# Order of the turns on SyncE's queue and the packet size of four v chunks in a fused attention and mixer kernel

## The chip, the cores and the metric

The kernel runs on one core of a Trainium2 chip. The metric is the device time of one execution in microseconds (us). A core has five engines that run their own instruction streams: TensorE (PE, with its weight loads PEld), VectorE (DVE), ScalarE (ACT), GpSimd (POOL) and SyncE (SP), which only issues transfers here. The transfers run on 16 DMA engines. In the profile the transfers that POOL issues are queue q0 (software_dynamic) and those that SP issues are queue q1 (hardware_dynamic).

## What is computed

Batch is 8, the sequence S is 3008, the model width is 256, the width of z is 64. First a gated attention without softmax, then a mixer over tokens and over channels:

```python
scores = (1.0 / S) * np.matmul(z, z.transpose(0, 2, 1))
attn = np.maximum(scores, 0.0) ** 2
x = u * np.matmul(attn, v)                       # S x 256 for each batch
h = np.maximum(x.transpose(0, 2, 1) @ w_tok1, 0.0) @ w_tok2
u2 = x + h.transpose(0, 2, 1)
out = u2 + np.maximum(u2 @ w_ch1, 0.0) @ w_ch2
```

Inputs and output are float32; the kernel computes in bf16 with float32 sums.

## The kernel before

**Tiles.** The sequence is cut into 24 tiles of 128 rows and these into 6 chunks of 4 tiles (`NG` = 6, `GK` = 4; the last chunk, `LAST` = 5, is short: 3 tiles and 64 rows). A block (b, q) is the attention of 512 query rows of batch b (`NQ` = 6 blocks for a batch). A block goes through 6 groups: group g multiplies the squared scores of 512 queries and key chunk g with chunk g of v. So the whole attention is a sequence of steps, numbered (b * NQ + q) * NG + slot; step 12 is the first group of the third block of batch 0.

**Scores.** PE makes scores (L457) in pairs of key tiles, ACT takes them out of PSUM with the ReLU into a tile named `at` (L495), DVE squares them in place (L503). There are 6 buffers for `at`. In batch 0 every block makes all its own scores. From batch 1 on, a score block off the diagonal is made once and used twice: as it is for block q, and turned, for block g. Turning it (a "flip", L554) is a transposing DMA on SP's queue from `at` to a tile named `fl`. An `at` buffer is free again once PE and its flip have read it.

**Turning by DMA.** SP also issues the transposing DMAs that turn z (`turn_z`, L141 and L145, from `zs` to `zT`; three for the second half), u (`turn_u`, L258, from `ur` to `uT`) and the gated result x (`turn_x`, L875, from `xT` to `x_pair`). The first chunks of batch 0's z are turned on PE, but chunks 2 and 3 by DMA (`turn_first_z`, L150, from `zr` to `zT`). SP takes its queue strictly in order, and each instruction waits there for what it needs. `turn_x` of block (b, q) needs the block's end: PE's sums, added and multiplied by u on DVE (L818, L838).

**Loading.** POOL issues every load that has to become bf16: v (L220), u (L248), z (L129), the weights w_tok1 (L267), w_tok2 (L277) and w_ch (L284, L289). POOL takes its queue in order, too. A one-column copy to a scratch tile (`after`, L124) serves as a gate: POOL stops at it until the named column has been written. One such gate stands ahead of the loads of batch 1's v, of all weights and of two chunks of u; it waits for the last column of batch 1's turned z (`zTs[1][:, KT, :1]`).

**v of batch 0.** It lies in three buffers of the ring `fl` (11 buffers, shared with `ur` and `uT` of batch 0's later blocks and with the flips). Buffer c // 2 holds chunks c, one after the other, so that each partition's part of a chunk, 4 rows of 256 bf16, is one run of 2 KB in the destination. `release("fl", ...)` counts a buffer free when both of its chunks have been used in batch 0's last block.

**Order.** Under a manual schedule the program writes instructions in the order that a planner in Python finds while the kernel is built. It keeps a clock for PE (`pe[0]`), ACT, DVE and SP with estimated durations, and at each turn picks the piece of work that can start first. `at_group(n, f)` hangs a load or a turn on step n: f is written out when the planner reaches that step. SP's part in it is `on_sp` and `push("sp", ...)`; the time that loads take from SP's transfers is guessed by `loading` and `shared`. The planner is not told how transfers share the DMA engines. The DVE sums of the mixer (`x_sums`, L912, that read `x_pair`; `token_sums`, L956, that read w_tok1) are pushed at estimated times after the turns and loads that they need.

On SP's queue, up to batch 1's flips, the written order before the change is: u(0,1), x(0,0), first half of batch 1's z (step 12), u(0,2) (step 13), x(0,1), u(0,3) and second half of z (step 14), u(0,4), u(0,5) (steps 15 and 16), x(0,2), and so on. The gate on POOL and the loads behind it start at step 15.

Of the kernel before, what the change touches and what calls it, by code (L numbers as in the profile page):

```python
# [9 lines left out]
BF16 = mybir.dt.bfloat16  # L10
# [3 lines left out]
P = 128  # L14
QW = 512
GK = 4
# [41 lines left out]
def kernel(  # L58
# [12 lines left out]
    B, S, D = u.shape  # L71
# [9 lines left out]
    NQ = (S + QW - 1) // QW  # L81
    NG = KT // GK
    LAST = NG - 1
# [4 lines left out]
    sb = ctx.enter_context(tc.tile_pool(name="sb", bufs=2))  # L88
# [25 lines left out]
    def rows_of(ap, c):  # L114

        n = full_tiles[c]
        return ap[c * QW:c * QW + n * P, :].rearrange("(p t) d -> p t d", t=n)

    def last_rows(ap):
        return ap[(KT - 1) * P:, :]  # L120
# [67 lines left out]
    def bank_pair(slot, name):  # L188

        if slot == RING and not last_psum:  # L190
            first.close()
            last_psum.append(ctx.enter_context(
                tc.tile_pool(name="last_psum", bufs=1, space=bass.MemoryType.PSUM)))
        pool = psum if slot < RING else last_psum[0]
        return pool.tile([P, 2, QW], F32, tag=f"ps{slot}", name=name, bufs=1)
# [12 lines left out]
    def load_v(b, c):  # L208
        if b == 0:

            if c // 2 not in v_first:
                v_first[c // 2] = sb.tile(
                    [P, 2, GK, D], BF16, tag="fl", name="v_sb", bufs=ROOM["fl"])
                live["fl"] += 1
                fl_free.pop(0)
            vt = v_first[c // 2][:, c % 2]
        else:
            vt = sb.tile([P, GK, D], BF16, tag="v", name="v_sb", bufs=NG)
        n = full_tiles[c]
        nc.gpsimd.dma_start(out=vt[:, :n, :], in_=rows_of(v[b], c))  # L220
        if n < GK:
            for r in range(2):
                nc.gpsimd.dma_start(
                    out=vt[r * TAIL:(r + 1) * TAIL, n, :], in_=last_rows(v[b]))
        vs[b, c] = vt
        v_in[b, c] = Done(pe[0] + 9.0 if b > 1 else 0.0)
        loading(LOAD)

    v_first, v_uses = {}, [[2] for _ in range(NG // 2)]

# [104 lines left out]
    def loading(us):  # L335
        loads[0] = max(loads[0], pe[0] + 1.0) + us
# [8 lines left out]
    ROOM = {"at": 6, "fl": 11, "xT": 9, "h2": 6, "us": 2}  # L345
# [48 lines left out]
    pe = [0.0]  # L394
# [164 lines left out]
    def release(name, uses, t=0.0):  # L559
        uses[0] -= 1  # L560
        uses[1:] = [max([t] + uses[1:])]
        if not uses[0]:
            live[name] -= 1
            if name == "at":
                at_free.append(uses[1])
            if name == "fl":
                fl_free.append(uses[1])
# [37 lines left out]
    def finished(blk, g):  # L605
        blk.parts[g] -= 1
        if not blk.parts[g]:
            _, _, name, uses = blocks.pop((blk.b, blk.q, g))
            release(name, uses, pe[0] + 0.2)
            if blk.b == 0 and blk.q == NQ - 1:  # L610
                release("fl", v_uses[g // 2], pe[0] + 0.2)

    def tails_ready(blk):

# [27 lines left out]
    def do_whole(start, g):  # L642
        blk = cur[0]
        begins = blk.g is None
        if begins:
            blk.g, blk.half = g, 0
            blk.todo.remove(g)
            blk.slot += 1
            blk.parts.setdefault(g, 2 if g == LAST else 1)
            n = grain(blk.b, blk.q, g)  # L650
            tiles = list(range(GK - 1 if g == LAST else GK))
            blk.steps = [(dh, tiles[i:i + n]) for i in range(0, GK, n) for dh in range(DT)]
        final = blk.slot == NG
        if begins:
            if final and not blk.tails:
                do_tails(blk, max(start, tails_ready(blk)))
                start = pe[0]
        dh, tiles = blk.steps[blk.half]
        start, end = on_pe(start, "full", len(tiles) * column_time(blk.W))
        for i in tiles:  # L660
            whole_matmul(blk, g, i, dh, final and i == tiles[-1])
        if final:
            acc_free[dh] = push(
                "dve", end + 0.21, 0.61, 0.75,
                lambda t, dh=dh: gate(blk, dh, blk.acc[dh], t), first=1,
                room=("xT",) if dh == 0 else lambda: (blk.b, blk.q) in xTs)
        blk.half += 1
        if blk.half == len(blk.steps):
            blk.g = None
            finished(blk, g)  # L670
            if final:
                end_block(blk)
                if blk.q == WHOLE - 1:
                    ring.append((acc_free[-1], RING))
# [71 lines left out]
    def do_half(start, g):  # L746
        blk = cur[0]
        if blk.whole:
            return do_whole(start, g)
        if blk.g is None:  # L750
            start_bundle(blk, g, start)
        g, dh, tiles = blk.steps[blk.half]
        blk.half += 1
        final = dh is not None and blk.slot == NG and not any(
            d == dh or d is None for _, d, _ in blk.steps[blk.half:])
        if dh is not None and blk.acc[dh] is None:
            blk.home[dh], free_at = take_slot()
            blk.acc[dh] = bank_pair(blk.home[dh], f"acc{dh}")
            start = max(start, free_at)
        start, end = on_pe(start, "half", len(tiles) * column_time(blk.W))  # L760
        for i in tiles:
            for h in range(2):
                av_matmul(blk, g, i, h if dh is None else dh, h, final and i == tiles[-1])
        if final:
            finish(blk, dh, end)
        if blk.half == len(blk.steps):
            blk.g = None
            for g in blk.bundle:
                _, _, name, uses = blocks.pop((blk.b, blk.q, g))
                release(name, uses, pe[0] + 0.2)  # L770
                used[blk.b, g] = used.get((blk.b, g), 0) + 1
                if blk.b == 0 and blk.q == NQ - 1:
                    release("fl", v_uses[g // 2], pe[0] + 0.2)
            if blk.slot == NG:
                end_block(blk)

# [154 lines left out]
    def take_slot():  # L931
        slot = min((s for s in ring if s[0].t is not None), key=lambda s: s[0].t)
        ring.remove(slot)
        return slot[1], slot[0].t
# [574 lines left out]
    def turn_next_z(b, half):  # L1509
        turn_z(zTs[b + 1], half)  # L1510
        on_sp(2.8 + 1.2 * half)

        for c in range(NG // 2 * half, NG // 2 * (half + 1)):
            turned[b + 1, c] = Done(pe[0] + 10.0)
        if half:
            turned[b + 1, NG // 2 - 1] = Done(pe[0] + 10.0)
# [4 lines left out]
    def at_group(n, f):  # L1521
        fetch.setdefault(n, []).append(f)
# [45 lines left out]
    for b in range(B):  # L1568
        base = b * NQ * NG
        for q in range(NQ):  # L1570
            m = b * NQ + q + 2
            if b == 0:
                if m < NQ:
                    at_group(base + NG, lambda m=m: load_u(m // NQ, m % NQ))
                late_turn = NQ * NG + 1 + 4 * (m - NQ) if m >= NQ else 2 * NG + (1, 2, 3, 4)[q]
                at_group(base + late_turn, lambda m=m: turn_u(m // NQ, m % NQ))
            elif m < 2 * NQ:
                ask_u(m, base + q * NG + 2)
        if b == 0:
            at_group(base + 2, lambda b=b: new_zT(b + 1))  # L1580
            for j in range(NG):
                at_group(base + 3 + j // 2, lambda b=b, j=j: load_z(b + 1, j))
                if j % 3 == 2:
                    at_group(base + 12 + 2 * (j // 3), lambda b=b, j=j: turn_next_z(b, j // 3))
        else:
            if b == 1:
                ask_z(2, base + HALF * NG - 1)
            if b + 1 < B:
                last, m = base + NQ * NG - 1, (b + 1) * NQ
                ask_u(m, last)  # L1590
                for j, c in enumerate(vorder):
                    at_group(last, lambda b=b, c=c, j=j: when_used(b, c, j))
                ask_u(m + 1, last)
                ask_u(m + 2, last)
                if b + 2 < B:
                    ask_z(b + 2, last)
                for k in range(3, NQ):
                    ask_u(m + k, last)
# [66 lines left out]
    items += [lambda c=c: ask_w_tok2(c) for c in range(NG)]  # L1665
    items += [lambda part=part: ask_w_ch(part) for part in range(4)]
    items += [lambda m=m: load_u(m // NQ, m % NQ) for m in (NQ, NQ + 1)]
    begin = 2 * NG + 3
    at_group(begin, lambda: after(zTs[1][:, KT, :1]))
    for k, item in enumerate(items):  # L1670
        at_group(begin + k * (NQ * NG - NG - begin + 1 + W_LATER) // len(items), item)
# [33 lines left out]
    while cur[0] is not None or heads or tails:  # L1705
        run_engines(pe[0])
        ask_some()
        t = pe[0]
        ta, g = next_half(t)
# [133 lines left out]
```

## Times and profile before

| | |
|---|---|
| time, median of 3 runs | 1132.12 us (1129.81 to 1133.4) |
| the profiled execution | 1130.13 us, of which 1128.3 are its span |
| PE busy | 1112.0 us, 99% of the span |
| DVE busy | 782.6 us, 69% |
| ACT busy | 654.1 us, 58% |
| POOL busy | 162.9 us, 14% |
| transferred | 165.52 MB, mean 147 GB/s |

Rows of a timeline give start, duration, engine, line, operation, tiles and count, and in brackets the idle time of the engine just before with what ended it. SPq rows are DMA issues: their start is when the queue came to them, their duration is the issue, not the transfer. "DMA to landing" is the time from an issue to its data's arrival (least, median, most). A row of a view by windows has the stretch, then busy time and count of each engine (PE, PEld, DVE, ACT, POOL), then the granted PE clock, then the busy share of the DMA engines (over 1 where packets overlap) and GB/s. A queue's row has packets, MB and the share of the 16 engines' time.

### The profile page before, as it was taken

The numbers are of one execution on the slowest core, as the hardware profiler recorded it, in microseconds if no ns is written. First come the engines' busy times: TensorE is split into PE (matmuls) and PEld (weight loads), VectorE is DVE, ScalarE is ACT, GpSimd is POOL, SyncE is SP. The second block draws the span as 40 slices with busy tenths as digits, with TensorE's granted clock in tenths as the row PEclk, the third lists the DMA queues.
The fourth block names the chain that finished last, engine by engine and source line by source line (L and its number), as shares of the span: only waits on it lengthen the run. The fifth ranks groups of instructions, "written<-read, shape, count | busy, mean of one in ns | idle before, by whom it ended". The sixth has DMA issues, their size and how long they took to land.

```text
span 1128.3 us, 26908 instructions
## 1 busy us (share of the span) xinstructions
PE 1112.0 (99%) x10965; PEld 676.1 (60%) x10965; DVE 782.6 (69%) x1849; ACT 654.1 (58%) x817; POOL 162.9 (14%) x388
## 2 busy tenths in 40 slices
PE   8999999999999999999999999999999999999998
PEld 3444465666557665576555765557655576556676
DVE  6888756875767757578566785667756777557774
ACT  7997535535855358545665456753666526753353
POOL 4140010221002110022100320003110120000000
PEclk9999999999999999999999999999999999999999
DMA  9699965688977879879697896957969779594223
GB/s 171 97 200 193 199 129 118 112 156 165 180 143 131 163 149 183 139 145 186 141 149 143 143 198 133 190 112 136 201 145 161 127 145 175 135 164 97 61 65 87
DMA packets 464620, 165.52 MB, mean 147 GB/s; under 512 B 433072, under 2 KB 446960, under 8 KB 464496
## 3 DMA queue, kind: packets, MB, share of 16 engines
q1 hardware_dynamic: 436640, 131.11, 58.2%
q0 software_dynamic: 27344, 32.32, 20.5%
q8 instruction: 85, 1.39, 0.5%
q10 hardware_dynamic: 512, 0.38, 0.1%
q14 instruction: 39, 0.32, 0.1%
HBM read 65.40 MB, written 24.64 MB: 80 GB/s over the span
## 4 chain that ended last, share of the span: by engine, by line
PE 89%; DVE 5%; DMA 4%; ACT 1%; issue 1%; SPq 0%; ACTq 0%; DVEq 0%
PE acc L684 37%; PE hp L1117 21%; PE xb L1245 9%; PE zb L1245 7%; PE sc L457 6%; PE a_ps L1017 3%; DMA fl<-at 3%; PE op L1331 3%; PE h_ps L1061 2%; DVE xT L1070 2%; ACT at L495 1%; PE first_acc L601 1%; DMA zT<-zr 1%; DVE at L503 1%; DVE res L1366 0%
## 5 line engine op out<-in xcount | busy, mean ns | idle before, releaser
L1155 ACT ACTIVATE h2pre<-hp 128x1024 bf16<-128x1024 f32 (+1 forms) x277 | 267.6, 1011 | 262.8 <-PE hp L1117 224.9
L684 PEld LDWEIGHTS <-v_sb 64*128 64x128 bf16 x4418 | 239.7, 94 | 217.6 <-issue 1.5
L684 PE MATMUL acc<-at,v_sb 64*128 64x512 bf16 (+1 forms) x2738 | 339.2, 374 | 0.0
L495 ACT ACTIVATE at<-sc 128x1024 bf16<-128x1024 f32 (+1 forms) x290 | 287.2, 1027 | 80.9 <-PE sc L457 58.4
L503 DVE TENSOR_TENSOR at<-at 128x1024 bf16<-128x1024 bf16 (+1 forms) x290 | 198.3, 688 | 113.2 <-ACT at L495 109.0
L1117 PE MATMUL hp<-xT,w_ch_sb 128*128 128x512 bf16 (+1 forms) x1152 | 270.6, 375 | 0.3
L684 PE MATMUL acc<-fl,v_sb 64*128 64x512 bf16 (+1 forms) x1680 | 192.0, 367 | 0.3 <-ACT at L495 0.3
L1117 PEld LDWEIGHTS <-w_ch_sb 128*128 128x128 bf16 x1152 | 105.9, 98 | 99.8 <-issue 2.7
L457 PE MATMUL sc<-zT 64*128 64x512 bf16 (+1 forms) x732 | 131.5, 359 | 7.8 <-ACT at L495 5.4
L1245 PEld LDWEIGHTS <-hsum 128*128 128x128 bf16 x1944 | 115.9, 98 | 20.1 <-issue 0.2
L1245 PEld LDWEIGHTS <-h2pre 128*128 128x128 bf16 x1458 | 88.8, 98 | 18.9
L812 ACT COPY cp<-acc 128x512 f32<-128x512 f32 (+1 forms) x94 | 54.9, 584 | 72.1 <-PE acc L684 59.7
L818 DVE TENSOR_TENSOR cp<-acc,cp 128x512 f32<-128x512 f32 (+1 forms) x94 | 63.5, 675 | 37.3 <-ACT cp L812 36.8
L1196 DVE TENSOR_TENSOR hsum<-h2pre 128x512 bf16<-128x512 bf16 (+1 forms) x132 | 53.0, 405 | 42.2 <-ACT h2pre L1155 36.7
L483 ACT ACTIVATE at<-sc 128x512 bf16<-128x512 f32 (+3 forms) x152 | 55.9, 443 | 44.9 <-PE sc L457 38.9
L457 PEld LDWEIGHTS <-zT 64*128 64x128 bf16 x732 | 42.5, 94 | 52.0 <-issue 12.2
L1245 PE MATMUL xb<-w_mix_sb,hsum 128*128 128x128 bf16 x972 | 68.6, 219 | 0.0
L534 DVE TENSOR_TENSOR at<-at 128x512 bf16<-128x512 bf16 (+3 forms) x152 | 41.6, 322 | 35.9 <-ACT at L483 35.8
L1282 DVE TENSOR_TENSOR ro<-xb,u_sb 128x256 f32<-128x256 f32 (+1 forms) x132 | 52.7, 399 | 17.2 <-PE xb L1245 16.2
L838 DVE TENSOR_TENSOR xT<-cp,uT 128x512 bf16<-128x512 f32 (+1 forms) x94 | 62.4, 664 | 0.6
L124 POOL CAST mark<-at 128x1 f32<-128x1 bf16 x24 | 8.0, 332 | 335.5 <-DVE at L503 335.5
L1070 DVE TENSOR_TENSOR xT<-xT,h_ps 128x1024 bf16<-128x1024 bf16 (+1 forms) x48 | 54.9, 1170 | 0.1
(88 smaller groups left out, 982.7 us busy)
## 6 DMA issues: line engine op xcount, KB each, us to landing
out_dram<-ro SPq DMA_DIRECT2D x37, 512.0 KB, 2.9
v_sb<-in_v_dram POOLq DMA_DIRECT2D x40, 256.0 KB, 5.0
ur<-in_u_dram POOLq DMA_DIRECT2D x40, 256.0 KB, 4.9
w_tok_sb<-in_moe_w_tok_dram POOLq DMA_DIRECT2D x10, 256.0 KB, 10.7
zs<-in_z_dram POOLq DMA_DIRECT2D x35, 64.0 KB, 3.8
at<-at SPq DMA_TRANSPOSE x114, 3.1
out_dram<-ro SPq DMA_DIRECT2D x7, 256.0 KB, 2.4
fl<-at SPq DMA_TRANSPOSE x105, 4.6
```

The source lines that it names most:

```text
L457: nc.tensor.matmul(sc[:, r, c0:c1], zT[h, k:k + P], zT[h, m + c0:m + c1], start=True, stop=True)
L483: nc.scalar.activation(a3[:, i, c0:c1], sc[:, r, c0:c1], ACT.Relu, scale=inv_S)
L495: nc.scalar.activation(view, sv, ACT.Relu, scale=inv_S)
L503: nc.vector.tensor_mul(view, view, view)
L684: nc.tensor.matmul(o, vs[blk.b, g][rows, i, dh * P:(dh + 1) * P], rhs, start=(dh, h) not in blk.begun, stop=stop, skip_group_check=True)
L812: nc.scalar.copy(cp[:, :W], acc[:, 1, :W])
L818: nc.vector.tensor_add(cp[:, :W], acc[:, 0, :W], cp[:, :W])
L838: nc.vector.tensor_mul(xT[:, dh, :full * P].rearrange("p (t s) -> p t s", s=P), acc[:, :full * P].rearrange("p (t s) -> p t s", s=P), uT[: ...
L1070: nc.vector.tensor_add(to, to, h[:, :, :n * P].rearrange("p h (s t) -> p h t s", t=n))
L1117: nc.tensor.matmul(hp[:, r, :W], w_ch1_sb[:, dc, cc * P:(cc + 1) * P], xT[:, dc, :W], start=(dc == 0), stop=(dc == DT - 1))
L1155: nc.scalar.activation(h2[:, :, :W], hp[:, :, :W], ACT.Relu)
L1245: nc.tensor.matmul(to[:, i * P:(i + 1) * P], lhs, weights[:, c2, :], start=(first_use and c2 == 0 and i == 0), stop=(c2 == CHT // 2 - 1), ...
```

## The change

Two things are changed. The layout of batch 0's v: chunks 0 and `LAST` now share a buffer, one after the other as before; chunks 1 and 2 share one, and chunks 3 and 4, and in these two buffers the rows of the two chunks alternate, so that a partition's part of a chunk is four runs of 512 bytes. The function that names the buffer, `v_place`, also serves the releases. And the steps at which turns are written out: u(0,2) to u(0,5) go from steps 13, 14, 15, 16 to 11, 12, 12, 13; the two halves of batch 1's z from steps 12 and 14 to 10 and 11; the gate and the loads behind it begin at step 12 in place of 15, and end at the same step as before.

```diff
     def load_v(b, c):
         if b == 0:
-            if c // 2 not in v_first:
-                v_first[c // 2] = sb.tile(
-                    [P, 2, GK, D], BF16, tag="fl", name="v_sb", bufs=ROOM["fl"])
+            k, half = v_place(c)
+            if k not in v_first:
+                v_first[k] = sb.tile([P, 2 * GK, D], BF16, tag="fl", name="v_sb", bufs=ROOM["fl"])
                 live["fl"] += 1
                 fl_free.pop(0)
-            vt = v_first[c // 2][:, c % 2]
+            if k == 0:
+                vt = v_first[k][:, half * GK:half * GK + GK]
+            else:
+                vt = v_first[k].rearrange("p (t r) d -> p t r d", r=2)[:, :, half]
...
+    def v_place(c):
+
+        return (0, int(c == LAST)) if c in (0, LAST) else (1 + (c - 1) // 2, (c - 1) % 2)
...
-                release("fl", v_uses[g // 2], pe[0] + 0.2)
+                release("fl", v_uses[v_place(g)[0]], pe[0] + 0.2)
...
-                late_turn = NQ * NG + 1 + 4 * (m - NQ) if m >= NQ else 2 * NG + (1, 2, 3, 4)[q]
+                late_turn = NQ * NG + 1 + 4 * (m - NQ) if m >= NQ else NG + (5, 6, 6, 7)[q]
                 at_group(base + late_turn, lambda m=m: turn_u(m // NQ, m % NQ))
...
-                    at_group(base + 12 + 2 * (j // 3), lambda b=b, j=j: turn_next_z(b, j // 3))
+                    at_group(base + NG + 4 + j // 3, lambda b=b, j=j: turn_next_z(b, j // 3))
...
-    begin = 2 * NG + 3
+    begin = 2 * NG
     at_group(begin, lambda: after(zTs[1][:, KT, :1]))
     for k, item in enumerate(items):
         at_group(begin + k * (NQ * NG - NG - begin + 1 + W_LATER) // len(items), item)
```

The release line stands in two places, in `finished` (L608) and in `do_half` (L773). The written order on SP's queue becomes: u(0,1), x(0,0), first half of z, u(0,2), second half of z, u(0,3), u(0,4), u(0,5), x(0,1), x(0,2), and so on.

More of the change, by code (lines that the diff above doesn't have):

```diff
@@ L772, in do_half @@
                 if blk.b == 0 and blk.q == NQ - 1:
-                    release("fl", v_uses[g // 2], pe[0] + 0.2)
+                    release("fl", v_uses[v_place(g)[0]], pe[0] + 0.2)
             if blk.slot == NG:
```

## The prediction

> **What bounds the kernel now.** I read the waits first, then the timeline around each. PE is busy nearly all of the span, so a change can win only where PE waits. The waits of PE in the first 160 us:
>
> ```profile
> PE sc L457 <- ACT at L495: 4.6, 3, 2.3
> PE sc L457 <- DMA zT<-zr: 1.6, 1, 1.6
> ```
>
> Both large ones are downstream of transfers. The first in time is the start: after four small products PE wants chunk 3 of z, which is still being turned, and ACT starves with it.
>
> ```profile
> 10.67 1.04 PE L601 MATMUL first_acc<-at,v_sb 128*128 128x512 bf16 x4
> 13.53 0.39 PE L457 MATMUL sc<-zT 64*128 64x512 bf16 x2 [1.61 <-DMA zT<-zr]
> 13.96 1.02 ACT L495 ACTIVATE at<-sc 128x1024 bf16<-128x1024 f32 x1 [1.47 <-PE sc L457]
> L150 SPq DMA_TRANSPOSE zT<-zr x2: 1203/1255/1307, 4.6 to 6.0; - x2
> DMA to landing us min/median/max: 4.8/6.1/7.5
> ...
> L220 POOL DMA_DIRECT2D v_sb<-in_v_dram x5: 532/548/693, 6.1 to 8.2; - x5
> DMA to landing us min/median/max: 4.5/7.4/8.6
> ```
>
> The turn issued at 6.0 took 7.5 us to land, the one issued at 4.6 took 4.8, among five loads of v issued from 6.1 to 8.2, the first of which landed in 4.5. The second is a hole at the start of batch 1, seen in PE's and in ACT's timeline, with the landing of the flips behind it:
>
> ```profile
> 109.20 0.39 PE L457 MATMUL sc<-zT 64*128 64x512 bf16 x2 [2.32 <-ACT at L495]
> 116.24 0.39 PE L457 MATMUL sc<-zT 64*128 64x512 bf16 x2 [1.87 <-ACT at L495]
> ...
> 108.13 1.94 ACT L495 ACTIVATE at<-sc 128x1024 bf16<-128x1024 f32 x2 [2.99 <-DMA fl<-at]
> 115.16 1.94 ACT L495 ACTIVATE at<-sc 128x1024 bf16<-128x1024 f32 x2 [2.34 <-DMA fl<-at]
> ...
> L554 SPq DMA_TRANSPOSE fl<-at x9: 1361/2782/6644, 87.6 to 120.3; - x9
> DMA to landing us min/median/max: 3.7/5.8/9.5
> ```
>
> PE waits for ACT, and ACT for an `at` buffer that a flip has not yet read: 2.32 + 1.87 = 4.2 us of PE hang on flips (the third wait, 0.4 us, does not). Why the flips are late is seen on SP's queue and POOL's:
>
> ```profile
> 26.43 1.23 SPq L875 DMA_TRANSPOSE x_pair<-xT  x1
> 27.85 2.54 SPq L141 DMA_TRANSPOSE zT<-zs  x2
> 30.49 1.26 SPq L258 DMA_TRANSPOSE uT<-ur  x1
> 42.22 1.23 SPq L875 DMA_TRANSPOSE x_pair<-xT  x1
> 43.55 1.26 SPq L258 DMA_TRANSPOSE uT<-ur  x1
> ...
> 47.60 1.19 SPq L145 DMA_TRANSPOSE zT<-zs  x1
> ...
> 87.59 6.64 SPq L554 DMA_TRANSPOSE fl<-at  x1
> 94.33 1.61 SPq L258 DMA_TRANSPOSE uT<-ur  x1
> ...
> 50.09 0.47 POOL L124 CAST mark<-zT 128x1 f32<-128x1 bf16 x1 [26.78 <-DMA zT<-zs]
> ...
> 33.00:43.00 10.00, 10.00 (x96) 4.78 (x94) 8.41 (x14) 9.41 (x12) 0.00 (x0) 1.00 0.01 2
> 50.00:95.00 45.00, 45.00 (x434) 22.05 (x432) 40.17 (x81) 41.50 (x50) 17.52 (x31) 1.00 1.21 185
> ```
>
> From 31.8 to 42.2 SP stands before x(0,1), which waits for the second block's end; the second half of z is queued behind it, POOL's gate waits for that until 50.09, and from 33 to 43 us the DMA engines do nothing (share 0.01). The loads then fill them from 50 to 95 (1.21), past the first flip at 87.59, whose issue alone takes 6.64 us where the least is 1.36.
>
> **The change, part by part.** *Packets of 512 bytes.* How a turn fares among loads is in the packets of both queues, first against large packets (83 to 85 us), then against small ones (87 to 89):
>
> ```profile
> q0 software_dynamic: 144, 0.38, 95.7%
> q1 hardware_dynamic: 144, 0.04, 13.3%
> ...
> q0 software_dynamic: 479, 0.24, 86.3%
> q1 hardware_dynamic: 492, 0.13, 47.1%
> ```
>
> In both the queues take turns one packet each. With q0's packets at 0.38 MB / 144 = 2.6 KB a turn gets 72 packets in a us, with 0.24 MB / 479 = 500 bytes it gets 246. The Trainium skill (DMA: Bandwidth & Descriptors, Queues, rings and completion order) says that a DMA engine round-robins between queues by packets, and that a packet is a run of some 9 to 17 descriptors; the trace agrees with the first and shows the switch at every 500 bytes, so not with the second. By the second, four rows would stay in one packet, and this term would be nothing.
>
> A turn here is 256-byte packets (0.13 MB / 492), and a 128 x 512 tile of bf16 is 512 of them. At 72 they take 7.1 us, which is the 7.5 above; at 246 they take 2.1. The turn before it lands at 4.6 + 4.8 = 9.4, beside chunk 0 of v, which stays in large packets; so this one would land by 9.4 + 2.1 = 11.5 in place of 13.5. PE wants it at 13.53 - 1.61 = 11.92, ACT at 13.96 - 1.47 = 12.49, so the wait goes, worth 1.47 us, since ACT then sets the pace. What is late next is chunk 1 of v. It lands at 6.1 + 4.5 = 10.6 now and yields more turns to the queue beside it when cut in 512 packets, so I put it at 10.6 to 11.6; PE wants it with the third of the four products at 10.67, at 11.1. I take 0.25 us off for that: **-1.2 us**. Ends: -1.6, and +0.6 where chunk 1 comes as late as the turn did, at 13.5 (then two products, four small ones and the scores follow it at 14.1 in place of 13.53).
>
> What the small packets cost in bytes, from a stretch of 2 KB loads and one of 512-byte loads (the z loads):
>
> ```profile
> 17.00:19.00 2.00, 2.00 (x13) 0.71 (x11) 1.39 (x3) 1.84 (x3) 1.99 (x4) 1.00 1.12 209
> 19.00:21.00 2.00, 2.00 (x11) 0.88 (x9) 1.39 (x2) 2.00 (x3) 1.31 (x4) 1.00 1.41 191
> 13.65 0.53 POOL L129 DMA_DIRECT2D zs<-in_z_dram  x1 [2.23 <-DMA v_sb<-in_v_dram]
> 64.21 0.72 POOL L277 DMA_DIRECT2D w_tok_sb<-in_moe_w_tok_dram  x1 [1.05 <-DMA v_sb<-in_v_dram]
> ```
>
> 209 against 191 GB/s: four chunks of 256 KB take 5.0 or 5.5 us, so what lies behind them comes 0.5 us later. POOL's issue of one run for each partition is 0.53 us, of two runs (w_tok2) 0.72; at about 0.25 more for four runs, 1 us in all, hidden because POOL then waits anyway until chunks of v land (2.23 us at 13.65). Both count nothing: a chunk is used in 8 products of 0.217 (1.04 - 0.39 over three), 1.73 us, and lands in 1.4. Without that cover they cost at most their 1.5 us.
>
> *The turns moved.* Seven issues go ahead of x(0,1): the three of z's second half (2.54 + 1.19), and u(0,3), u(0,4), u(0,5) (1.26 each); the seventh is u(0,2), already ahead. From 31.8 they take 3.7 + 3.8 + gaps, to 39.6, and x(0,1) is due at 42.22, so it isn't held up. The u loads are in: POOL's idle 26.78 us before 50.09 put its last issue before 23.3, and that is a piece of u that lands in 6.0, at 29.3:
>
> ```profile
> ur<-in_u_dram POOLq DMA_DIRECT2D x1, 32.0 KB, 6.0
> ```
>
> The last turn of z is issued at about 34.3 and lands 2.4 us later (47.60 to 50.0 now), so the gate opens near 36.7 in place of 50.09, 13.4 us sooner. 45 us of loads then end near 82 in place of 95, ahead of the first flip (87.59 - 1.2). The flips then issue in 1.36 us and land in some 4; each follows its own squares, and the 4.2 us go. Ends: 0 (the flips stay late) and -4.6 (the 0.4 too). I take **-4.2**, nearest to the rows that name flips alone.
>
> What is queued behind now? x(0,1) goes out at 41 into the loads, not ahead of them. Turns of x among loads, and the sum on DVE that reads x(0,1):
>
> ```profile
> L875 SPq DMA_TRANSPOSE x_pair<-xT x6: 1232/1232/1247, 26.4 to 96.0; - x6
> DMA to landing us min/median/max: 2.7/7.2/16.3
> 63.77 0.28 DVE L912 TENSOR_TENSOR d_pair<-x_pair 128x256 bf16<-128x256 bf16 x1
> ```
>
> At the worst, 16.3, it lands at 57.3; DVE reads it at 63.77 - 1.2 = 62.6. Cost nothing, 5 us of cover; DVE runs in order, so beyond that every us would stop the squares. The releases by `v_place` keep chunk 0's buffer one group longer (16 products, about 3 us) in block (0,5), before the flips; nothing while a flip needs no buffer sooner. The loads' last step in the plan is the same; the token sums come about two groups earlier on DVE, which is busy 40.2 of the 45 us from 50 to 95.
>
> *Sum*: -1.2 - 4.2 = -5.4. On the profiled execution 1130.13 - 5.4 = 1124.7; that one lies 2.0 below the median, and the forecast is for the median: 1132.12 - 5.4 = **1126.7 us**. Its own range is 1123.8 to 1129.
>
> **The rivals.** *Half a hole.* The flips are late for a second reason: SP's row at 94.33 shows one u turn between flips, and each u chunk of batch 1 is loaded among them. For: nine flips up to 120 us take 5.8 in the middle, and the loads were done at 95. Against: these were queued behind the first. One of the two waits stays: 1132.12 - 1.2 - 2.1 = 1128.8.
>
> *The start gives nothing.* Chunk 1 comes as late as chunk 3 of z did, because it shares its buffer row by row with chunk 2 and PE is made to wait for both, or because packets hold several rows, as the page above has it. Then 1132.12 - 4.2 = 1127.9. Against the second: 479 to 492.
>
> *The planner gives it back.* Due times moved by two steps order every later piece of work anew. The waits of PE after 150 us:
>
> ```profile
> 150.00:1128.00 978.00, 970.38 (x9751) 607.28 (x9748) 664.87 (x1639) 536.77 (x685) 125.45 (x310) 1.00 0.76 143
> ```
>
> 978.0 - 970.4 = 7.6 us; half as much again is +3.8, so 1130.5. Nothing in the trace speaks for a sign.
>
> *Slower: x(0,1) lands after DVE wants it.* Place: the first L912 on x(0,1), at 62.6. u(0,5) and x(0,1) now both go out into the start of the loads; if x takes twice the worst, 32.6 us, it lands at 73.6 and DVE, then ACT, then PE stand for 11 us, less some 2 that six `at` buffers hold: 1126.7 + 9 = 1136. It decides above 21.6 us of landing, and the sign turns near 30. Against: of six turns none took over 16.3.
>
> **How the numbers follow.** Forecast 0.48, half a hole 0.17, start gives nothing 0.09, planner 0.13, slower 0.13. A measurement of this kernel tells about 0.3% from no change, 3.4 us: faster is below 1128.7, slower above 1135.5. Faster: nearly all of the forecast (0.44), half of the start case (0.05), a little of half a hole (0.03): 0.52. Slower: the last rival and 0.01 of the planner: 0.14. The rest, 0.34, is the same. The runs before spread by 1.8 us to either side, so the range goes from 1123.5 (both terms at their ends, and spread) to 1133.5, which leaves out the slower case and little below.
>
> **What would show it.** Right: PE's wait on zT<-zr gone and ACT's idle 1.47 with it; the L150 turn landing in about 5 us; POOL's gate near 37 us; no idle DMA from 33 to 43; q0 quiet by about 83; the first flip issued in under 2 us; no ACT wait on fl<-at between 100 and 120. Wrong: a wait of first_acc on v_sb near 11 us; ACT still waiting for fl<-at; a DVE wait on x_pair near 62; more PE idle after 150 us than 7.6.

## The result and the profile after

The changed kernel takes 1126.02 us, median of 19 runs (1122.7 to 1129.08); the kernel before, beside it, 1132.12, also of 19 (1127.47 to 1138.0). The ratio is 0.9933 with a 95% interval of 0.9918 to 0.9948, so the kernel is faster, by 0.67%. The profiled execution took 1123.19 us, of which 1121.4 are its span (1130.13 and 1128.3 before). Lines of the changed kernel stand 3 to 7 lower in the file: L457 is now L464, L495 is L502, L554 is L561, L258 is L265, L875 is L882, L220 is L223.

These are TensorE's waits in the first 160 us. The 4.6 us on ACT and the 1.6 us on zT<-zr are gone; the 0.8 us on v_sb is chunk 0, which the change leaves alone:

```profile
PE wp L205 <- DVE zero L1504: 1.2, 1, 1.2
PE first_acc L608 <- DMA v_sb<-in_v_dram: 0.8, 1, 0.8
PE h_ps L1068 <- DVE xT L1077: 0.5, 1, 0.5
PE sc L464 <- ACT zT L1685: 0.2, 1, 0.2
```

The start, in the timeline of PE:

```profile
11.96 0.39 PE L464 MATMUL sc<-zT 64*128 64x512 bf16 x2
```

and of ACT:

```profile
10.63 2.85 ACT L502 ACTIVATE at<-sc 128x1024 bf16<-128x1024 f32 x3 [1.07 <-PE sc L464]
```

The group of z's two turns in it (issue, least, median and most in ns, then the landing):

```profile
L150 SPq DMA_TRANSPOSE zT<-zr x2: 1194/1256/1317, 4.4 to 5.8; - x2
...
DMA to landing us min/median/max: 5.3/5.5/5.7
```

and the group of the four interleaved loads of v:

```profile
L223 POOL DMA_DIRECT2D v_sb<-in_v_dram x4: 740/749/920, 6.0 to 8.2; - x4
```

The scores that stood at 13.53 behind a wait of 1.61 stand at 11.96 without one: 1.57 us. The second turn of z takes 5.3 us where it took 7.5, the first 5.7 where it took 4.8. ACT is no longer starved for 1.47 us in one piece, but it still idles 1.07 ahead of 10.63. An issue of four runs for each partition costs POOL 0.75 us against 0.53.

SP's queue in the timeline:

```profile
26.28 2.54 SPq L141 DMA_TRANSPOSE zT<-zs  x2
...
30.34 2.54 SPq L141 DMA_TRANSPOSE zT<-zs  x2
32.98 1.18 SPq L145 DMA_TRANSPOSE zT<-zs  x1
34.25 5.17 SPq L265 DMA_TRANSPOSE uT<-ur  x3
40.65 38.14 SPq L882 DMA_TRANSPOSE x_pair<-xT  x4
86.02 1.64 SPq L561 DMA_TRANSPOSE fl<-at  x1
...
91.42 9.02 SPq L561 DMA_TRANSPOSE fl<-at  x3
100.53 1.34 SPq L265 DMA_TRANSPOSE uT<-ur  x1
101.97 2.66 SPq L561 DMA_TRANSPOSE fl<-at  x1
```

POOL's, with the gate and the second of the loads of u that fall among the flips:

```profile
37.37 0.30 POOL L124 CAST mark<-zT 128x1 f32<-128x1 bf16 x1 [14.57 <-DMA zT<-zs]
...
105.50 0.53 POOL L255 DMA_DIRECT2D ur<-in_u_dram  x1 [3.94 <-DMA uT<-ur]
```

The group of the flips:

```profile
L561 SPq DMA_TRANSPOSE fl<-at x9: 1403/2232/5720, 86.0 to 116.5; - x9
...
DMA to landing us min/median/max: 3.8/5.3/7.9
```

And three stretches, where the last two numbers are the DMA engines' share and GB/s:

```profile
31.00:37.00 6.00, 6.00 (x58) 2.83 (x56) 4.65 (x8) 6.00 (x8) 0.00 (x0) 1.00 0.70 109
37.00:82.00 45.00, 45.00 (x430) 22.02 (x429) 39.17 (x70) 42.11 (x50) 16.91 (x30) 1.00 1.18 186
82.00:90.00 8.00, 8.00 (x82) 4.00 (x78) 7.81 (x20) 6.91 (x9) 1.40 (x1) 1.00 0.57 71
```

The gate opens at 37.4 in place of 50.1, the stretch without transfers is gone, the loads fill 37 to 82, and the first flip goes out in 1.64 us. But the flips as a whole are hardly quicker: they still land in 5.3 us (5.8 before), and one issue still takes 5.72. And the order on the queue is another than before among the flips too: after the flip at 86 come three flips, then a turn of u, where it was two flips and the turn. That isn't in the diff; it is the plan that put it there.

To see where the 6.94 us of span come from, compare the starts of the same loads of v's weights on TensorE in both traces; either kernel has 4466 of them, and a negative number is earlier than before. It is -1.57 us at the 16th and still at the 664th (106.29 us before); -4.05 at the 668th, behind the first wait of the hole; -6.78 at the 720th, behind the second; -7.5 at the 3300th (754 us before); -7.93 at the end of the loads of v, and 1.0 of it is given back in the tail. So the start gives 1.57, the hole 2.48 + 2.73 = 5.2, and all that comes later 0.2. These are two single executions, 2.0 us under the median of the kernel before and 2.8 under that of the changed one.

### The profile page after: what moved, and what is told of

The parts are those of the page before. It is cut to its first block, busy times and chain, and to the rows that moved or that the text cites. A ratio compares the mean times of both kernels' runs of the same rounds, so it can differ in the third digit from the quotient of the medians.

```text
span 1121.4 us, 26909 instructions
## 1 busy us (share of the span) xinstructions
PE 1110.3 (99%) x10965; PEld 676.5 (60%) x10965; DVE 782.4 (70%) x1849; ACT 654.1 (58%) x817; POOL 164.7 (15%) x388
## 4 chain that ended last, share of the span: by engine, by line
PE 91%; DVE 4%; DMA 2%; SPq 1%; ACT 1%; issue 1%; POOL 0%; ACTq 0%; DVEq 0%; POOLq 0%
PE acc L691 39%; PE hp L1124 22%; PE xb L1252 9%; PE zb L1252 7%; PE sc L464 6%; PE a_ps L1024 3%; PE op L1338 3%; PE h_ps L1068 2%; DVE xT L1077 2%; DMA fl<-at 1%; PE first_acc L608 1%; DMA v_sb<-in_v_dram 1%; DVE res L1373 0%; ACT at L502 0%; DVE ro L1289 0%
## 5 line engine op out<-in xcount | busy, mean ns | idle before, releaser
L502 ACT ACTIVATE at<-sc 128x1024 bf16<-128x1024 f32 (+1 forms) x290 | 287.2, 1027 | 74.9 <-PE sc L464 56.8
L464 PE MATMUL sc<-zT 64*128 64x512 bf16 (+1 forms) x732 | 131.6, 359 | 1.0 <-ACT at L502 0.7
L464 PEld LDWEIGHTS <-zT 64*128 64x128 bf16 x732 | 42.3, 94 | 43.7 <-issue 4.9
```

The source lines that it names most:

```text
L464: nc.tensor.matmul(sc[:, r, c0:c1], zT[h, k:k + P], zT[h, m + c0:m + c1], start=True, stop=True)
L502: nc.scalar.activation(view, sv, ACT.Relu, scale=inv_S)
```

## The experiments

Twelve kernels, in three series, each with the kernel before beside it. The table has, for each profiled execution: PE's lead at the 16th and the 720th load of v's weights (that is, behind the start and behind the hole) and the change of the span, all against the profiled execution of before (negative is earlier or shorter); the landing of the last load of the batch (the second of u, L248 or L255); the landing of the third and of the fifth flip; and the ratio of the timed runs to before's, with its interval. "Turn" tells whether the turn of u stands ahead of the fourth flip or behind it.

```
                     16th   720th    span  loads  flip3  flip5  turn    ratio
before                 -       -       -    95.4  108.0  115.1  ahead
after               -1.57   -6.78   -6.94   82.3  100.7  106.7  behind  0.9933 [0.9918, 0.9948]
e1 packets          -0.43   -0.17   +2.84   94.4  107.5  114.9  ahead   0.9979 [0.9954, 1.0004]
e2 turns            -1.09   -6.30   -5.09   81.4  101.5  107.7  behind  0.9921 [0.9894, 0.9948]
e6 1 KB             -0.86   -6.07   -6.83   82.8  101.8  108.1  behind  one run
e8 chunks 1, 2      -1.94   -7.16   -4.27   80.9  100.8  107.1  behind  one run
e12 chunks 3, 4     -1.30   -6.51   -7.09   82.1  101.7  107.9  behind  one run
e3 z ahead          -1.68   -3.28   +1.43   84.8  104.2  111.8  ahead   0.9968 [0.9941, 0.9996]
e4 u ahead          -1.75   -2.05   -3.91   83.1  100.5  111.4  ahead   0.9948 [0.9920, 0.9975]
e5 step 15          -1.69   -2.34   +0.07   81.9  101.1  111.1  ahead   0.9953 [0.9930, 0.9977]
e7 loads held       -1.51   -4.93   -3.81   88.0  101.5  110.1  ahead   0.9981 [0.9953, 1.0008]
e9 loads held more  -1.73  +13.80  +14.75  108.6  118.6  124.8  behind  1.0106 [1.0060, 1.0152]
e10 one turn ahead  -1.80   -2.49   -2.00   82.3  100.1  111.1  ahead   0.9940 [0.9916, 0.9964]
e11 before, behind  -1.35   -2.63   -3.66   93.1  106.4  111.1  behind  0.9965 [0.9939, 0.9992]
```

**The two halves of the change, e1 and e2.** e1 keeps the layout of v and puts the three steps back; e2 keeps the steps and puts the layout back.

```diff
-late_turn = ... else NG + (5, 6, 6, 7)[q]
+late_turn = ... else 2 * NG + (1, 2, 3, 4)[q]
-at_group(base + NG + 4 + j // 3, ...)
+at_group(base + 12 + 2 * (j // 3), ...)
-begin = 2 * NG
+begin = 2 * NG + 3
```

```diff
-            k, half = v_place(c)
...
-            if k == 0:
-                vt = v_first[k][:, half * GK:half * GK + GK]
-            else:
-                vt = v_first[k].rearrange("p (t r) d -> p t r d", r=2)[:, :, half]
+            vt = v_first[c // 2][:, c % 2]
```

> The v layout alone, every turn and the loads' gate at their old steps. If the two edits act apart: PE's wait of 1.6 us on zT<-zr goes and nothing else, the gate on POOL stays near 49 us, the hole near 107 to 116 us keeps its PE idle of about 4.6 us, and the time is 1.6 us under the kernel before (ratio 0.9986). If the layout acts through the releases of its buffers, so that flips get room sooner, the hole shrinks as well and the gain is 3 us or more.

> The turns and the gate moved alone, v in runs of 2 KB. If the two edits act apart: PE waits 1.6 us for zT<-zr near 12 us as in the kernel before, the gate opens near 38 us, the first flip is issued in under 2 us, the hole is gone, and the time is 5.2 us under the kernel before (ratio 0.9954). If the early start of chunk 3 of z is what puts the turns ahead of x(0,1) in time, the gate opens later than 40 us and part of the hole stays.

e1 keeps the hole (-0.43 behind the start, -0.17 behind the hole) and isn't told from before. e2 has the whole of the hole's gain and takes as long as the changed kernel, and in it the start too is 1.09 us ahead, though its packets are the old ones. TensorE's scores behind chunk 3 of z, in the timeline of e1:

```profile
12.34 0.60 PE L608 MATMUL first_acc<-at,v_sb 128*128 128x512 bf16 x2 [1.65 <-DMA v_sb<-in_v_dram]
13.10 0.39 PE L464 MATMUL sc<-zT 64*128 64x512 bf16 x2
```

and of e2:

```profile
10.72 0.60 PE L457 MATMUL sc<-zT 64*128 64x512 bf16 x4 [1.06 <-DMA zT<-zr]
...
12.45 0.39 PE L457 MATMUL sc<-zT 64*128 64x512 bf16 x2
```

In e1 chunk 1 of v came late: this is the wait on v_sb that the prediction named as the sign against it, in one execution of small packets. The start differs between executions by about what it was to gain.

**How much the packets give: e6, e8, e12.** Runs of 1 KB in place of 512 bytes (e6); small packets for chunks 1 and 2 alone (e8), for chunks 3 and 4 alone (e12). The edits, in this order (e6's load and products index the buffer to match):

```diff
-                vt = v_first[k].rearrange("p (t r) d -> p t r d", r=2)[:, :, half]
+                vt = v_first[k].rearrange("p (t r e) d -> p t r e d", r=2, e=2)[:, :, half]
```

```diff
-            if k == 0:
+            if k != 1:
                 vt = v_first[k][:, half * GK:half * GK + GK]
```

```diff
-            if k == 0:
+            if k != 2:
                 vt = v_first[k][:, half * GK:half * GK + GK]
```

> As the changed kernel, but chunks 1 and 2, and 3 and 4, alternate by pairs of rows, so that runs are 1 KB. If the queues take turns packet by packet, the second turn of z lands between 11.2 (512 bytes) and 13.5 us (2 KB), near 12, and PE waits 0 to 0.6 us for it; chunk 1 of v lands no later than the 11.2 us of the changed kernel. If only runs of 512 bytes let a turn through, it lands at 13.5 us and the wait of 1.6 us is back.

> The changed kernel with chunks 3 and 4 of v in large packets again, chunks 1 and 2 alone in packets of 512 bytes. Theory (what the start gains is that chunk 3 of z is turned beside small packets, and of these chunks 1 and 2 are in the queue at 6 to 11 us): chunk 3 of z lands by 11.2 to 11.8, no wait of PE on zT above 0.3, PE 1.2 to 1.6 us ahead of the kernel before at 16 us, span as the changed kernel's, 1120 to 1124. Rival (the start varies from execution to execution by as much as the packets give): chunk 3 of z lands past 12.2, PE under 0.9 ahead.

> The changed kernel with chunks 1 and 2 of v in large packets again, chunks 3 and 4 alone in packets of 512 bytes. Theory (what the start gains comes from chunks 1 and 2, beside which chunk 3 of z is turned): chunk 3 of z lands past 11.8, PE 0 to 1.1 us ahead of the kernel before at 16 us, as with large packets alone. Rival (chunks 3 and 4 matter, or the start varies by itself): 1.4 to 2 us ahead.

e6 lies between, at 0.86. e8 has the largest lead of all, 1.94; chunk 3 of z landed at 10.90. e12 has 1.30 (z at 11.85), a little over what was expected of large packets, and so has e11 below, with the old layout, 1.35. Taken together, by the packets in which chunks 1 and 2 came: 512 bytes in nine executions, 1.57, 0.43, 1.94, 1.68, 1.75, 1.69, 1.51, 1.73, 1.80, median 1.69; 2 KB in four (before, e2, e12, e11) 0, 1.09, 1.30, 1.35, median 1.2. The medians differ by 0.5 us, but the ranges overlap, 0.43 to 1.94 against 0 to 1.35. Within the last series, which has two of each, it is 1.73 and 1.80 against 1.30 and 1.35: 0.45. The landing of chunk 3 of z itself tells the two apart better: 10.04 to 11.17 us in eight of the nine and 13.03 in e1, against 11.85 to 13.49 in the four, and 11.71 with 1 KB. The zero is the profiled execution of before. It had the latest start of the fourteen, and the prediction read its 1.47 us from it.

**Which turns: e3 and e4.** e3 moves z and the loads and leaves u's steps; e4 moves u, with z and the loads at their old steps.

```diff
-late_turn = ... else NG + (5, 6, 6, 7)[q]
+late_turn = ... else 2 * NG + (1, 2, 3, 4)[q]
```

```diff
-at_group(base + NG + 4 + j // 3, ...)
+at_group(base + 12 + 2 * (j // 3), ...)
-begin = 2 * NG
+begin = 2 * NG + 3
```

> As the changed kernel, but u(0,2) to u(0,5) are turned at their old steps, so that u(0,3) to u(0,5) stand behind x(0,1) again. If the start of the loads is all that counts, the gate opens at 36 us or a little before, the hole is gone and the time is that of the changed kernel within 1 us. If the u turns had to go ahead as well, they now land late, in the midst of the loads (11 to 17 us each): DVE would wait for uT at the end of a block (near 62, 75 or 87 us), 1 to 5 us in all.

> The changed kernel with the second half of z turned at its old steps, behind x(0,1); only the turns of u stay ahead. Theory (the hole is set by when the loads of batch 1 begin, and these wait for the last turn of z): the gate on POOL opens near 50 us, loads run until 92 to 95, the first flip's issue is long again (above 4 us), ACT waits for fl<-at between 100 and 120, and PE is level with the changed kernel up to 100 us and 4 to 5 us behind it after 117: some 1130.5 us. Rival (the hole comes from single turns of u and x that stand among the flips, or from the planner's order): no hole, 1126 us.

Neither made the queue that it was meant to make. In e3 the turns of u still went out ahead of x(0,1), in e4 the second half of z did too. SP's queue in e4:

```profile
35.03 3.64 SPq L141 DMA_TRANSPOSE zT<-zs  x2
38.73 1.24 SPq L145 DMA_TRANSPOSE zT<-zs  x1
40.46 1.24 SPq L882 DMA_TRANSPOSE x_pair<-xT  x1
```

and the gate, on POOL:

```profile
41.24 0.19 POOL L124 CAST mark<-zT 128x1 f32<-128x1 bf16 x1 [18.13 <-DMA zT<-zs]
```

So both are close to the changed kernel up to the flips, the loads end at 83 and 85, and the first wait of the hole is gone or small; and yet they lose 3.5 and 4.7 us against it behind the hole. What they share with before is the place of one turn of u among the flips. e3 loses another 4.7 us between the 720th load of weights and its end; why is not shown. In e3 x(0,1), out at 40.95 among the loads, took the longest of all turns of x, as the group of its turns shows:

```profile
L882 SPq DMA_TRANSPOSE x_pair<-xT x6: 1232/3656/14927, 24.8 to 91.3; - x6
...
DMA to landing us min/median/max: 2.9/12.0/26.2
```

It landed at 67.2, and DVE did not wait for it: the plan has the first sum on it at 70.3 there.

**When the loads begin: e5, e7, e9.** All keep the steps at which the change writes the turns. e5 sets the first step back to 15; e7 sets it to 16 and adds a gate on the newest squares; e9 has sixty copies at the gate in place of one, which leaves the order on SP's queue as it is.

```diff
-    begin = 2 * NG
+    begin = 2 * NG + 3
```

```diff
-    begin = 2 * NG
+    begin = 16
     at_group(begin, lambda: after(zTs[1][:, KT, :1]))
+    at_group(begin, lambda: after(recent[0]))
```

```diff
-    at_group(begin, lambda: after(zTs[1][:, KT, :1]))
+    at_group(begin, lambda: [after(zTs[1][:, KT, :1]) for i in range(60)])
```

> The changed kernel with the first step of the plan for the loads back at 15 (12 in the change); the turns stay ahead. POOL has nothing of its own to wait for there, so theory: the gate still opens at 36 to 38 us, loads end by 83, no hole, 1126 us (1124 to 1128). Rival (the first step counts by itself, because the plan places the loads' issues and the waits in them): the gate opens near 48, loads end past 90, 1129 to 1131.

> The changed kernel with every turn where the change put it, but the loads of batch 1 held back on POOL until the work of step 16 (some 50 us), so that they begin about when they began before. Theory (late loads alone make the hole): loads end past 93 us, flips issue long, ACT waits for fl<-at, PE is 3 to 5 us behind the changed kernel after 117: 1130 us. Rival (the queue's order makes it: turns that still stood in SP's queue behind x(0,1) made the flips late): no hole, 1126 us, whatever the loads do.

> The changed kernel with 60 small copies of one column on GpSimd in place of one ahead of the loads of batch 1, so that the loads begin some 11 to 14 us later, near where they began before; SP's queue and every other engine keep the order of the changed kernel. Theory (the first half of the hole is the late loads: they run into the first flip): loads end past 91 us, the first flip takes over 3 us to issue, the first wait of PE near 109 is back with 1.5 to 2.5 us, the second is not: PE 2 to 3 us behind the changed kernel at 124, 1128.5 us. Rival (turns that stand ahead of the flips are enough): no wait, 1126 us.

e5 went as expected up to the flips (loads end at 81.9) and then lost 4.4 us to the changed kernel behind the hole: a miss in the trace, with the turn of u ahead again. That execution took 1130.2 us and is the slowest of e5's ten; their median, 1126.96, lies where it was expected. e7's loads began at 44.1, not at 50, and ended at 88.0; the first flip still went out in 1.68 us, and the wait that came was the second one, 1.4 us, with the turn of u ahead there as well. Its profiled execution is 3.81 us shorter than that of before, but its timed runs, at 0.9981, are not told from before. In e9 the copies took 0.45 us each, twice what was reckoned, so the loads began at 64.7 and ended at 108.6. POOL's timeline of e9:

```profile
37.15 27.27 POOL L124 CAST mark<-zT 128x1 f32<-128x1 bf16 x60 [14.93 <-DMA zT<-zs]
```

SP's queue in it:

```profile
85.87 10.62 SPq L561 DMA_TRANSPOSE fl<-at  x1
107.33 1.27 SPq L265 DMA_TRANSPOSE uT<-ur  x1
```

And PE's waits in the first 160 us:

```profile
PE acc L691 <- DMA fl<-at: 10.6, 1, 10.6
PE sc L464 <- ACT at L502: 6.7, 1, 6.7
```

That is far more than before's delay, and the cost with it: the first flip landed only at 104.7, the turn of u behind it waited for its own load, and PE stood 6.7 us for ACT and 10.6 more behind the next flip. PE's granted clock fell in that idle time, too, and stood at 0.50 from 104 to 122 us. Two stretches in which PE is busy throughout, at 119 and at 125 us (the clock is the third number from the end):

```profile
119.00:122.00 3.00, 3.00 (x16) 1.23 (x14) 0.00 (x0) 0.88 (x1) 0.00 (x0) 0.50 1.38 149
125.00:128.00 3.00, 3.00 (x32) 1.54 (x28) 2.54 (x6) 2.94 (x4) 0.00 (x0) 1.00 0.84 75
```

At half the clock 16 products take as long as 32 at the full one. From 117.0, where PE starts again, to 122 that is an estimated 2.5 us of e9's loss which is no wait. Over all kernels the issue of the first flip goes with the end of the loads: 1.6 us where they end between 80.9 and 88.0 (2.5 in e3, 84.8), 6.4 to 6.6 where they end between 93.1 and 95.4, 10.6 at 108.6.

**The place of one turn: e10 and e11.** e10 is the changed kernel with the second turn of u of batch 1 one step earlier, e11 the kernel before with that turn one step later.

```diff
-late_turn = NQ * NG + 1 + 4 * (m - NQ) if m >= NQ else ...
+late_turn = NQ * NG + 1 + 4 * (m - NQ) - (m == NQ + 1) if m >= NQ else ...
```

(e11 has `+ (m == NQ + 1)` there.)

> The changed kernel with one turn of u (the second of batch 1) one step earlier, so that in SP's queue it stands ahead of the fourth flip and not behind it. TensorE, VectorE, ScalarE and GpSimd run the same instructions in the same order. Theory (the second half of the hole hangs on this one place: the turn lets the next load of u go out before the fifth flip, and the fifth flip then lands among its packets): the fifth flip lands past 110 us where it lands at 106.7 in the changed kernel, ACT waits 2 to 4 us for fl<-at, PE is level with the changed kernel up to 112 us and 2.8 to 4.5 behind it at 124: 1129 us. Rival (that half opens for the late loads, or by the plan of the other engines): no wait, within 0.5 us of the changed kernel up to 300 us.

> The kernel before with that same turn of u one step later, behind the fourth flip; everything else is as before, so the loads are late. Theory (two causes, one for each half of the hole): the first wait of PE (2.3 us near 109) stays, the second (1.9 us near 116) goes or is under 0.5, PE 1.5 to 2.3 us ahead of the kernel before at 124 us: some 1130 us. Rival (late loads make both): both waits stay, 1132 us.

e10 is level with the changed kernel through the first wait (-4.88 against -4.65 at the 688th load of weights), and 4.3 us behind it at the 720th. SP's queue in e10:

```profile
98.15 1.27 SPq L265 DMA_TRANSPOSE uT<-ur  x1
99.51 4.78 SPq L561 DMA_TRANSPOSE fl<-at  x2
104.46 5.30 SPq L265 DMA_TRANSPOSE uT<-ur  x1
```

POOL's load of u:

```profile
101.54 0.53 POOL L255 DMA_DIRECT2D ur<-in_u_dram  x1 [0.20 <-issue]
```

ACT's timeline, and behind it PE's:

```profile
111.23 1.94 ACT L502 ACTIVATE at<-sc 128x1024 bf16<-128x1024 f32 x2 [3.78 <-DMA fl<-at]
```

```profile
112.30 0.61 PE L464 MATMUL sc<-zT 64*128 64x512 bf16 x2 [2.90 <-ACT at L502]
```

The turn at 98.15 frees u's buffer, so the next load of u goes out at 101.54 where it went out at 105.50, in the same moment as the fifth flip (101.24), and that flip takes 9.9 us to land (111.1) where it took 4.7. ACT starts at 111.23 on the buffer that this flip has read. e11 shows the reverse: the first wait is left, the second gone. Its queue:

```profile
86.24 6.42 SPq L554 DMA_TRANSPOSE fl<-at  x1
...
95.46 10.48 SPq L554 DMA_TRANSPOSE fl<-at  x3
```

and the only wait of PE in the hole:

```profile
107.61 0.39 PE L457 MATMUL sc<-zT 64*128 64x512 bf16 x2 [2.08 <-ACT at L495]
```

The same order stands in all fourteen traces. Where the turn is behind the fourth flip, the fifth flip is issued 2.2 to 3.7 us ahead of the second of the loads of u among the flips and lands in 3.75 to 4.9 us. Where the turn is ahead, the flip is issued 0.3 to 0.8 us ahead of that load and lands in 6.3 to 9.9 us.

One step of one turn, without any of the change, brings the time to 0.9965 of the time before (0.9939 to 0.9992). In e10 the timed runs lose less than its profiled execution does: its median is 1.0 us over the changed kernel's, its ratio 0.9940 against 0.9933, and the intervals overlap. e4 and e5, with the turn ahead as well, stand at 0.9948 and 0.9953. By the ratios these three are 0.8 to 2.3 us slower than the changed kernel, inside the intervals. So the second wait is shown in single executions, and what it costs on average is not. One execution of each kernel was profiled; the changed kernel's is the third fastest of its 19. No kernel here is told from the changed one as faster.

## Why the prediction was right, and where it was not

*The start, -1.2.* The signs came: no wait on zT<-zr, a turn in about 5 us, POOL's issue at 0.75 as estimated, no new wait on chunk 1. The profiled execution gained 1.57. But the step that made the term, "At 72 they take 7.1 us, which is the 7.5 above", does not hold. The 72 packets in a us were read at 83 to 85 us. In the profiled execution of before the two queues move, from 9.5 to 10.5 us and then from 10.5 to 12.6:

```profile
q0 software_dynamic: 69, 0.11, 79.0%
q1 hardware_dynamic: 401, 0.10, 48.1%
...
q0 software_dynamic: 93, 0.19, 131.2%
q1 hardware_dynamic: 28, 0.01, 6.0%
```

Some 400 packets of the turn pass in one us beside 69 of the loads, and the landing at 13.49 waits for the few that are left. So it was luck that 7.1 met 7.5. The step also took one execution for the kernel: other executions with 2 KB packets start 1.1 to 1.35 us earlier than that one. Chunk 3 of z does land sooner beside small packets, but how is open, and by the medians PE gains some 0.5 us from it; the rest of the 1.57 is the spread of the start. The sign of a wait for chunk 1 came once: e1 shows it, with 1.65 us. By the Trainium skill (DMA: Bandwidth & Descriptors, Queues, rings and completion order), as weighed in the prediction, the packets would give nothing. The landings, 10.04 to 11.17 in eight of nine against 11.85 to 13.49, speak for a little. No timed run settles it: e1, with the packets alone, is not told from before, nor e2, without them, from the changed kernel.

*The hole, -4.2.* 5.2 us closed. The size was short because the sum left out the third wait (0.42) and because rows understate each wait: the last product before it is drawn 0.38 us long, though products follow one another in 0.217, so each hides some 0.16. With both it is 2.32 + 0.42 + 1.87 + 3 x 0.16 = 5.1.

The mechanism was half right. That the loads end before the first flip, and that this is what the turns ahead of x(0,1) bring, was shown: gate at 37.4 (36.7 foretold), loads out of the way by 82.3 (82), first flip under 2 us, third flip 7.3 us earlier, the first wait gone, and back, larger, when the loads are held (e9). The step "the flips then issue in 1.36 us and land in some 4; each follows its own squares, and the 4.2 us go" fell for the second wait. The flips issue in up to 5.72 us and land in 5.3, because loads of u still fall among them, as the rival of half a hole said. That wait hangs on whether the fifth flip is out by 2 us or more before the second of these loads, and so on the place of one turn of u. The change did move that turn, but through the plan, which no line of the diff tells, and e5 undoes it with one number that was expected not to matter. So it was luck that the second wait went. The rival had the right mechanism for it. What its outcome would have been in time is open: e10's execution is 4.3 us behind the changed kernel at the 720th load, its timed runs 1.0 in the median.

*Costs put at nothing.* x(0,1) took 17.4 us in the changed kernel, a little over the worst turn of before, and DVE had no wait for it. The slower rival's limit, 62.6, was no limit: the plan moved the first sum on x(0,1) to 66.0 (70.3 in e3, where the turn took 26.2 us, past the point from which the rival was to decide). Releases and the fuller POOL queue cost nothing that shows.

*The planner.* PE's idle after 150 us is 8.0 us where it was 7.6:

```profile
150.00:1121.00 971.00, 963.01 (x9706) 604.12 (x9704) 661.99 (x1636) 534.67 (x683) 123.69 (x306) 1.00 0.76 143
```

The rest of the kernel gave nothing and cost next to nothing here. Between the kernels it varies more: from the 720th load of weights to the end e8 loses 2.9 us and e3 4.7, and e4 gains 1.9. The forecast for the median, 1126.7, so lies 0.7 from 1126.02 with one term too large by some 0.7 (1.2 for 0.5) and the other too small by 1.0, both read from single executions; that they nearly cancel is luck. The low end of the prediction's range, 1123.5, is not what its terms give: 1132.12 - 1.6 - 4.6 - 1.8 = 1124.1.

## What to carry to other kernels

When a planner writes the order of a queue, compare that order before and after as a whole: a due time moved at one place changed the place of a turn some 60 us later, and in the profiled executions half of the closed hole hung on it. A stall read from one profiled execution is one draw; before a term is built on a wait near the start, see whether the same wait stands in a second execution. Late transfers add up along a queue, so ask for each consumer which single transfer it waits for (here the third flip for the first wait, the fifth for the second), and what can go out just ahead of that one.

## What the runs showed of the hardware that was not expected

A load that starts among flips can slow both for 2 to 3 us. In the changed kernel the load of u issued at 92.57 is followed by a flip whose issue takes 5.72 us, and the DMA engines in the stretch from 94.5 to 97 us look like this (the row of packets, then the two queues with packets, MB and their share of 16 engines):

```profile
DMA packets 135, 0.13 MB, mean 50 GB/s; under 512 B 82, under 2 KB 82, under 8 KB 135
q0 software_dynamic: 53, 0.11, 67.8%
q1 hardware_dynamic: 82, 0.02, 3.6%
```

That is 50 GB/s, where the same engines move 204 from 55 to 57.5 us. Each packet of the load takes 0.678 x 16 x 2.5 / 53 = 0.51 us, though little else is under way; from 55 to 57.5 it is 0.98 x 16 x 2.5 / 257 = 0.15. The kernel before has the same at its first such load, 36 GB/s from 100.5 to 102.5 us. In all fourteen traces the third flip, which goes out next to that load, takes 5.1 to 6.2 us to issue where the least is 1.36, and here which flip it is decides whether TensorE waits. It does not happen at every load: in the changed kernel 49 flips are issued while a load of POOL's is on its way, and four of them take more than 4 us to issue; of the 56 issued without one none takes more than 3.51. Why it happens, no run shows.
